# A gated linear attention followed by a feed-forward block: the same turns of 44 generators in another sequence

## The chip, the core and the metric

The kernel runs on one core of one Trainium2 chip, in one launch. Time is device microseconds of that core; lower is better. The engines are named as in the profile: PE (TensorE matmuls; PEld its weight loads), DVE (VectorE), ACT (ScalarE), POOL (GpSimd) and SP (SyncE, whose queue issues nearly all DMAs). They run unsynchronized, each through its own list of instructions in program order, and wait for one another by semaphores.

## The reference

```python
# q, k, v, alpha: (4, 8, 768, 48) = batch, heads, time, head dim
for t in range(S):
    state = alpha[:, :, t, :, None] * state + einsum('bhd,bhe->bhde', k[:, :, t], v[:, :, t])
    y[:, :, t] = einsum('bhd,bhde->bhe', q[:, :, t], state)
x = y.transpose(0, 2, 1, 3).reshape(B, S, H * D)          # (4, 768, 384)

mu, var = mean(x), variance(x)                            # over the 384 columns
xn = (x - mu) / sqrt(var + 1e-06) * g_ln
out = x + maximum(xn @ w_ch1, 0.0) @ w_ch2                # 384 -> 1536 -> 384
```

All of it is float32, but the two weight matrices arrive as 64-bit floats, which the kernel rounds on the chip.

## The kernel before

**Tiling.** Time is cut into 6 chunks of 128 steps. One attention is one chunk of one batch, so there are 24, lettered `a` to `x` (chunk 0 is `a` to `d`, chunk 5 is `u` to `x`). The gates are handled as running sums of logarithms inside a chunk (chunk 0) or half a chunk of 64 steps (the others), so that the recurrence becomes matmuls: the prefix sum (L348 for chunk 0, L355 else), exponentials of it and of its negative (L358, L359), q and k scaled by them (L363, L365), transposed by TensorE (L422, attentions `a` to `l`) or by DVE and a pass through DRAM (L404, L150, L416, `m` to `x`), the scores (L435, L450) under a mask (L459, L464), the update of the state (L479, with L488, L492 on DVE and L494 on POOL) and the output (L505, L515). Then x is stored to DRAM (L539), normalised (L543 to L557) and transposed, by TensorE (L573) for chunks 0 and 1, by DVE and DRAM else (L563, L150, L568).

In L355 each half of the time steps is one matmul of 64 rows by 64 columns of the array: an even batch sends half h to output half h, an odd batch sends the halves crosswise. The PE writes two records for one float32 matmul, so one such turn has four.

**Feed-forward.** Chunk 0 goes through plain matmuls: hidden (L598, ReLU L601) and second product (L610). Chunks 1 to 5 use a scheme with fewer block products (15 instead of 18 for each half of the hidden stage, 20 instead of 24 for the second), which needs sums of blocks made beforehand: of w1 (`combine_first`, L845), of the normalised input of a chunk (`combine_x`, L870), of w2 (`combine_weights`, L675) and of the hidden blocks (`combine_hidden`, L704). A hidden product is L901, and its results are spread by ACT copies (L913), DVE adds (L917 to L930), POOL adds (L915 to L928) and a ReLU (L932, or L940 afterwards). A product of the second stage is L722; its results go into the output tile `ob` by L736, L739, L742, L746, and `send` (L589) stores it. Some products go on accumulating in the PSUM bank of an earlier one; in the hidden stage 13 follows 1 and 0 follows 13 (`JOINS`), and the products come in the order of `FIRST`, which ends in 1, 8, 13, 4, 0. All matmul outputs share 6 PSUM banks.

**What sets the order.** Each piece of work is a Python generator that issues a few instructions and yields; such a step is one turn. A string of 1543 letters, `ORDER`, written out by hand or by a program outside the kernel, says whose turn comes next, and nothing rearranges it afterwards:

```python
with tc.manual_schedule():
    for turn in ORDER:
        next(turns[turn], None)
```

So the string fixes the order of instructions on every engine and of the DMAs on SP's queue. The letters: `a` to `x` attentions; `A` to `H` the rounding of the eight pieces of the weights (four of w1, then four of w2; a piece's last turn loads the piece after next); `Y`, `Z` the hidden stage of chunk 0, `P`, `Q` its second stage; `S`, `W`, `X`, `N` the sums of blocks of w1, w2, input and hidden; `M` the products of chunks 1 to 4 (hidden and second) and the second stage of chunk 5; `V` the hidden products of chunk 5; `R` the ReLUs; `O` the loads of x into the output tiles.

Of the kernel before, what the change touches and what calls it, by code (L numbers as in the profile page):

```python
# [25 lines left out]


ORDER = (
    "acaaababcaaabcbadbcadcaacbbbbaaabcdedcafbbcccdacbAaafebaceafcbcddcfefadebabefaAc"
    "ccdfedffcefeedffffffffddeebBbbgbhgdgghAaiabAddbdbcddhhgddidfjggYYcccgYiYYAedefcg"  # L30
    "YgjdeefeechZeiZfhijfiihhBehjBiBZihBZZhhhhhhhhhYYlZZYCfZZgfCZgZejYYiCgYkfggjfjjjj"
    "YklDZjjjjjghjkjjghkhDiihhDZZZZjlfeCgeiiehDkfikYYYYkeYlkgllEllhYighEmZlligYYkkYjh"
    "ZSYinhYSlEljnEmihlllflOnllFFjikgkZZZlZjnZZjnjFhkjjemnjfnQkGkkfegilQfSSSkGfSSlFml"
    "gkmmmPihPjlngkkmmhGglPiHSghXniQHkPXXHSSSOXllPXllooWSPppoXoSlllQjnnlnnnnoonnpSmnn"
    "mmkXOXXommXPppjmipXQnWOpOSnoQomSpWkmOmQlmSnkWnmkQMMMMMMMMiMMkMMMMMnWMMMMWpllMMMM"
    "MPMMMMnrWnpppppppppqnoMWonMrpOGrqorWWWoMrrroooMkMMWrjMMMMMMMMMMRMmMMMMRMRMqpMMjq"
    "pMOjmRnpRMMMpMiqpRqRpoRqNMoMMMtMNNRpkMNiNMMMMMnqRNmmmNMoMMMMMNNMMNsjNNNMMrqMMMMn"
    "MMMMMMoorrrprrprWrrXMpXXXXqqqqtsMNMMMpotoMNMNMXXrqrXtptmXMMMMMMMMMMMMMXXtttsMnss"
    "MMMMMsqsqsMMpsMMOMMMMMMMqrrMMMMMMMooMMRMMMqMnrMMMMMMMMMMMrRRRMMMvMMMMttOtttuqtOr"
    "tttstossrRvpnsssRRRRNvuMMMNqMMMvRMrMstrOvuNmvvtqsvrrosrtNMNNNpNrNqMMMMMMMuNssMMs"  # L40
    "ssMuurNuuMMNMMMMNOXXXXXXXtMMtMXrMXMMMxwtMMMNMNNwxtttwwwXMtMwMMMMMsMMMMMMMtMMMXMM"
    "MMMMMMMMMMMMMMMuvtqttvvvvvvvrOwvOuvwxuvuxxxquuRMMMwMMMMMMMMMMMMMMRRRMMMMMMMMMMMM"
    "MvvvqxxxxusxxxxxxRxwwwxRRRRwwMuRuqsqMMNNNMMMuuutMuuuNxxMOuwxNNxvNwwwwsNNuvvvvNNN"
    "vNvtMMMMMMMMMMMvHMMMxMXXXXXXXXXMXMMMXMMxxxMMMMNNMMwwNMMvwwwxwxxMMMMMMMMMMMMMMMMM"
    "MMMMMMMMMMMMMMMMMMMMMMMMMMMMMMxORRMMMMMMRMMMMMMMMMMMROOxxXvRRRXRRRNMXXMMMXXMMXVO"
    "NXMMMNNNNNNNNNNNXXMVVMMMMXMVVVVVVVVVVVVVVVVVVVMVVVMMMMMMMVVVVVVVVVVVVVVVVVVVMMVV"
    "VVVVVVMMMMMMMVMVVNNVVVMRNRRRRRVRRMRMMVNNOMMMMMMOMRONNNNNMNMMMMNNNMMMMOMMMMMMMNMN"
    "MMMMNMMNNMMMMMMMMMMMMMM"
)


# [951 lines left out]
```

## Time and profile before

| | before |
|---|---|
| median of 3 runs | 418.63 us |
| lowest and highest run | 416.97 and 420.4 us |
| the profiled execution, its own time | 416.17 us |
| its span, first to last instruction | 414.4 us |
| mean granted TensorE clock in it | 1.0 |
| TensorE waiting for DVE, three waits | 2.8 us |
| moved by DMA | 61.26 MB |

The profile is of one execution. A line of the timeline or of the chain begins with the start in us from the span's first instruction and a duration in us; then engine, line of the code, operation, output and inputs by the program's names, and how many instructions were merged (x4). Numbers in square brackets are the engine's idle time ahead of it and what ended it. The chain of work that ended last is followed back from the last instruction to what released it, or to the instruction before it on its engine.

### The profile page before, as it was taken

The page shows a single profiled execution, that of the slowest core. Times are in us where ns is not written, and L with a number is a line of the kernel's source. Part 1 is how long each engine was busy: PE and PEld are TensorE (multiplying, and loading weights), DVE is VectorE, ACT ScalarE, POOL GpSimd, SP SyncE. Part 2 cuts the span into 40 slices and gives each one's busy share as a digit, 9 for nine tenths or more (in the row PEclk, how much of TensorE's full clock was granted, in tenths as well). Part 3 has the DMA queues.
Part 4 walks back from the last instruction along what each step waited for, and adds up shares of the span by engine and source line. Part 5 has one row for each costly group of instructions (what it writes and reads, how often), then busy time and mean ns, then how long its engine had stood idle before and what let it go on. Part 6 is the DMA issues. An engine that isn't in the chain of part 4 may idle for free.

```text
span 414.4 us, 11452 instructions
## 1 busy us (share of the span) xinstructions
PE 408.5 (99%) x4617; PEld 354.9 (86%) x4617; DVE 292.5 (71%) x555; ACT 217.0 (52%) x521; POOL 119.7 (29%) x134
## 2 busy tenths in 40 slices
PE   7999999999999999999999999999999999999997
PEld 5878888866568889998889998899998889999996
DVE  4798989999997978597268873579533298125754
ACT  5797668783354675245684345773353643245110
POOL 1011022221012571143380254250226321525200
PEclk9999999999999999999999999999999999999999
DMA  8989959879878576946776768636234200000301
GB/s 282 292 240 278 305 125 313 237 153 264 219 138 269 133 159 116 217 106 143 168 139 160 192 165 214 122 49 137 96 62 119 68 1 2 19 0 24 111 21 58
DMA packets 134051, 61.26 MB, mean 148 GB/s; under 512 B 90559, under 2 KB 130882, under 8 KB 133998
## 3 DMA queue, kind: packets, MB, share of 16 engines
q1 hardware_dynamic: 133848, 60.37, 57.1%
q8 instruction: 36, 0.59, 0.6%
q10 hardware_dynamic: 150, 0.17, 0.1%
q14 instruction: 17, 0.14, 0.1%
HBM read 43.12 MB, written 17.39 MB: 146 GB/s over the span
## 4 chain that ended last, share of the span: by engine, by line
PE 96%; DVE 1%; DMA 1%; issue 0%; SPq 0%; DVEq 0%
PE hps L901 32%; PE ops L722 31%; PE hps L598 8%; PE ops L610 8%; PE yps L515 5%; PE tps L422 3%; PE aps L450 3%; PE ups L479 3%; PE lps L355 2%; DMA rq<-in_q_dram 1%; PE aps L435 1%; PE yps L505 1%; PE xps L573 1%; DVE eq L870 1%; PE lps L348 0%
## 5 line engine op out<-in xcount | busy, mean ns | idle before, releaser
L901 PE MATMUL hps<-sum,w 128*128 128x256 f32 x192 | 46.3, 383 | 0.0
L901 PEld LDWEIGHTS hps<-sum,w 128*128 128x128 f32 x192 | 35.7, 190 | 6.3 <-ACT u L913 1.7
L722 PE MATMUL ops<-w,hT 128*128 128x192 f32 x224 | 40.5, 326 | 0.0
L746 ACT COPY u<-ops 128x192 f32<-128x192 f32 x30 | 9.5, 316 | 54.7 <-PE ops L722 54.6
L722 PEld LDWEIGHTS ops<-w,hT 128*128 128x128 f32 x224 | 37.3, 190 | 0.3
L742 POOL TENSOR_TENSOR ob<-ob,u 128x192 f32<-128x192 f32 x32 | 20.5, 650 | 57.9 <-ACT u L746 33.1
L494 POOL TENSOR_TENSOR mid<-mid,gate 112x192 f32<-112x192 f32 x20 | 12.0, 602 | 76.8 <-DMA gate<-row 35.9
L901 PE MATMUL hps<-xT,w 128*128 128x256 f32 x136 | 33.3, 380 | 0.6 <-DVE xT L870 0.6
L598 PE MATMUL hps<-xT,w 128*128 128x256 f32 x144 | 33.8, 384 | 0.0
L913 ACT COPY u<-hps 128x512 f32<-128x512 f32 x32 | 18.7, 584 | 28.0 <-PE hps L901 22.1
L610 PE MATMUL ops<-w,hT 128*128 128x384 f32 x96 | 32.6, 491 | 0.0
L913 ACT COPY hT<-hps 128x512 f32<-128x512 f32 x40 | 23.3, 585 | 12.3 <-PE hps L901 11.9
L901 PEld LDWEIGHTS hps<-xT,w 128*128 128x128 f32 x136 | 25.7, 190 | 4.3 <-PE ops L722 0.9
L598 PEld LDWEIGHTS hps<-xT,w 128*128 128x128 f32 x144 | 26.2, 190 | 3.7 <-DVE w L258 0.2
L722 PE MATMUL ops<-ws,sum 128*128 128x192 f32 x160 | 28.6, 327 | 0.0
L610 PEld LDWEIGHTS ops<-w,hT 128*128 128x128 f32 x96 | 17.7, 190 | 11.7 <-issue 0.6
L722 PEld LDWEIGHTS ops<-ws,sum 128*128 128x128 f32 x160 | 26.4, 190 | 0.6 <-ACT few L546 0.6
L736 DVE TENSOR_TENSOR ob<-ops,ob 128x192 f32<-128x192 f32 x40 | 13.1, 351 | 17.1 <-PE ops L722 10.2
L940 ACT ACTIVATE hT<-hT 128x512 f32<-128x512 f32 x40 | 22.9, 621 | 2.0 <-DVE hT L920 1.5
L722 PE MATMUL ops<-ws,hT 128*128 128x192 f32 x128 | 23.4, 326 | 0.0
L722 PE MATMUL ops<-more,sum 128*128 128x192 f32 x120 | 22.2, 328 | 0.0
L722 PEld LDWEIGHTS ops<-ws,hT 128*128 128x128 f32 x128 | 21.3, 190 | 0.1
(225 smaller groups left out, 1028.1 us busy)
## 6 DMA issues: line engine op xcount, KB each, us to landing
ws<-in_moe_w_ch_dram SPq DMA_DIRECT2D x8, 1152.0 KB
vn<-in_v_dram SPq DMA_DIRECT2D x12, 384.0 KB
kept<-x SPq DMA_DIRECT2D x24, 192.0 KB
ob<-kept SPq DMA_DIRECT2D x24, 192.0 KB
rows<-rj SPq DMA_DIRECT2D x48, 96.0 KB
out_dram<-ob SPq DMA_DIRECT2D x18, 192.0 KB
xrows<-xt SPq DMA_DIRECT2D x64, 48.0 KB
xT<-xrows SPq DMA_DIRECT2D x16, 192.0 KB
```

Of the source, the lines that this page charges most:

```text
L422: nc.tensor.transpose(tps[:, p], qk_of(c, b)[:, i, p].rearrange("p a b -> p (a b)")[:, :R], ident)
L450: nc.tensor.matmul(pair[o][halves[i if o else 1 - i], p, s], k_of[rs, p, s], q_of[rs, p, s], start=True, stop=True)
L479: nc.tensor.matmul(up[h, p], qk_of(c, b)[ts, 1, p, i, :D], vn[ts, i, p], start=True, stop=True)
L515: nc.tensor.matmul(yps[j][halves[s], i, p], of, by, skip_group_check=True, start=not (cross and k), stop=k == 1 or not cross)
L598: nc.tensor.matmul(hps, w1[:, f, j * P:(j + 1) * P], xT_of[0][:, f, bs], start=(f == 0), stop=(f == NF - 1))
L610: nc.tensor.matmul(ops_of[b], hT_of[c][:, j, b], w2[:, j], start=(j == 0), stop=(j == NJ - 1))
L722: nc.tensor.matmul(acc, lhs[:, j], rhs[:, j], start=j == 0 and n not in FOLLOWS, stop=j == NT - 1 and n not in FOLLOWS.values(), skip_grou ...
L736: nc.vector.tensor_add(x, acc, x)
L742: getattr(nc.vector if c + 1 == NCB else nc.gpsimd, f"tensor_{op}")(x, x, y)
L901: nc.tensor.matmul(acc[:, i], w, b, start=n not in JOINS and i == 0, stop=n not in JOINS.values(), skip_group_check=True)
L913: nc.scalar.copy(out=copied[n], in_=acc)
L940: nc.scalar.activation(out=x, in_=x, func=AFT.Relu)
```

## The change

The string `ORDER` is replaced by another with the same number of every letter, so every generator issues the same instructions, in the same order within itself, on the same engines and into the same pools of buffers. What differs is how the generators' turns are interleaved, and with it the order of each engine's instructions and of the DMAs. Nothing else in the file is touched.

```diff
--- before.py
+++ after.py
@@ -26,26 +26,26 @@
 
 
 ORDER = (
-    "acaaababcaaabcbadbcadcaacbbbbaaabcdedcafbbcccdacbAaafebaceafcbcddcfefadebabefaAc"
-    "ccdfedffcefeedffffffffddeebBbbgbhgdgghAaiabAddbdbcddhhgddidfjggYYcccgYiYYAedefcg"
-    "YgjdeefeechZeiZfhijfiihhBehjBiBZihBZZhhhhhhhhhYYlZZYCfZZgfCZgZejYYiCgYkfggjfjjjj"
-    "YklDZjjjjjghjkjjghkhDiihhDZZZZjlfeCgeiiehDkfikYYYYkeYlkgllEllhYighEmZlligYYkkYjh"
-    "ZSYinhYSlEljnEmihlllflOnllFFjikgkZZZlZjnZZjnjFhkjjemnjfnQkGkkfegilQfSSSkGfSSlFml"
-    "gkmmmPihPjlngkkmmhGglPiHSghXniQHkPXXHSSSOXllPXllooWSPppoXoSlllQjnnlnnnnoonnpSmnn"
-    "mmkXOXXommXPppjmipXQnWOpOSnoQomSpWkmOmQlmSnkWnmkQMMMMMMMMiMMkMMMMMnWMMMMWpllMMMM"
-    "MPMMMMnrWnpppppppppqnoMWonMrpOGrqorWWWoMrrroooMkMMWrjMMMMMMMMMMRMmMMMMRMRMqpMMjq"
-    "pMOjmRnpRMMMpMiqpRqRpoRqNMoMMMtMNNRpkMNiNMMMMMnqRNmmmNMoMMMMMNNMMNsjNNNMMrqMMMMn"
-    "MMMMMMoorrrprrprWrrXMpXXXXqqqqtsMNMMMpotoMNMNMXXrqrXtptmXMMMMMMMMMMMMMXXtttsMnss"
-    "MMMMMsqsqsMMpsMMOMMMMMMMqrrMMMMMMMooMMRMMMqMnrMMMMMMMMMMMrRRRMMMvMMMMttOtttuqtOr"
-    "tttstossrRvpnsssRRRRNvuMMMNqMMMvRMrMstrOvuNmvvtqsvrrosrtNMNNNpNrNqMMMMMMMuNssMMs"
-    "ssMuurNuuMMNMMMMNOXXXXXXXtMMtMXrMXMMMxwtMMMNMNNwxtttwwwXMtMwMMMMMsMMMMMMMtMMMXMM"
-    "MMMMMMMMMMMMMMMuvtqttvvvvvvvrOwvOuvwxuvuxxxquuRMMMwMMMMMMMMMMMMMMRRRMMMMMMMMMMMM"
-    "MvvvqxxxxusxxxxxxRxwwwxRRRRwwMuRuqsqMMNNNMMMuuutMuuuNxxMOuwxNNxvNwwwwsNNuvvvvNNN"
-    "vNvtMMMMMMMMMMMvHMMMxMXXXXXXXXXMXMMMXMMxxxMMMMNNMMwwNMMvwwwxwxxMMMMMMMMMMMMMMMMM"
-    "MMMMMMMMMMMMMMMMMMMMMMMMMMMMMMxORRMMMMMMRMMMMMMMMMMMROOxxXvRRRXRRRNMXXMMMXXMMXVO"
-    "NXMMMNNNNNNNNNNNXXMVVMMMMXMVVVVVVVVVVVVVVVVVVVMVVVMMMMMMMVVVVVVVVVVVVVVVVVVVMMVV"
-    "VVVVVVMMMMMMMVMVVNNVVVMRNRRRRRVRRMRMMVNNOMMMMMMOMRONNNNNMNMMMMNNNMMMMOMMMMMMMNMN"
-    "MMMMNMMNNMMMMMMMMMMMMMM"
+    "acaabaabaaaccbcbbdabcaadcabbcbcdbcabecfaadaecdebeacaabfAeadcefcbbacbeffafaddbedd"
+    "fefafAdddecffbdgbbgfhfffbccgfAafbgbifAgccddbeigeadhjgghYYhBYgeidfcheAddeYfjhiceY"
+    "dchcheedgYfciidecehBdihfeZjZjZihjhhBBZBhChhhhjijjZfhjjZZfYZZlCgYfkYhgifgYkfZCeZY"
+    "geCkgYYljYfDjjgjOjkjjjghYhhZiDYkihYZkilZZkDYhYZkjSjkileifgfDiYEljlkhgEleYZlhjYgl"
+    "jfilFnYiZlgllllOEjgYlfhiFSlglgnZhZgkhnhjikFZjkkjiZPElSmhSgFfnfnnZkkghljQZSemlhGe"
+    "mSnkXGmkjkOmXlimiGQkmHSSPHQPnlPlmmHkkWlnPSolSXPOXjllXoQSXnnSoWnnSiXnnponSnXmimml"
+    "oppQjXmoQMmppMPomQMWXpkMMnkMnpMoSWMjSMnWSmPMnXmMMoOmWinMMMMllkMpMMpMnQOnkMMMMMmM"
+    "lMrMWlWMnrpMORpRkppjrpnppiprMoMqMMMMMMMrMoorWWWMMrMMoMjmlRoMMROjMMmMonMMMopRMpMM"
+    "MMRrRoRpqrlMNmNNMMMNMqqpkNqqNMqMMMpWMRNMMRMMMonMMMNqNMpMNpNqtpNWsMMXopiNMMMMMMMp"
+    "MmMMnXMrMrrrnrNrrNrqoqXtqsXrMtoXMNMXXMXMtMsotMMMMsMqtoMMXMtXMMnpMqMrMMMqXMMMMsMq"
+    "MqrMOMMMMMspmqMMMoMMsMMtMnMMMMMovMOMMMsmMMMRpsGMruqtMMqMrMqMRMMMMMMrRttrtpMtttRt"
+    "qtstORvRspRrtsouMRMNMmrMrsvMNNNvMuMMqONssMnNsrmRMsRtuuvMuotNNtpMMvuMrMMMMMNNNntM"
+    "trpvMMMsuMrMMsNMNXMMMMwMXMXNMqNXXvMMXxMuvMMNXtMwMMtXMMMMMwMwMMrtXOMwMMMMsXMMOXMw"
+    "qMMMvvtvvwvvvMvstuuuxMMrMMxMsMtMMMxMuMMwMxRORMsMMMxMMtqMMRMMsMtMMsMMMMRuMMxMRwMM"
+    "MMvMxMxuvvxxxRxOvsxxRxRNxMMwNwMMRxwNxvwwRvMNxsxxuMvMMNvwtNMNvuxMMxtNMMMNMxxMxNrM"
+    "NwwuMMNMwuxMxvMNvqXwuMXvMMMXMXMMMMMNvNwMXMMMNvuXXMXMMMMMwMMwMMMwMxMXMMMXMwuMMMMM"
+    "xMMXMMMMMMuuxMvMMwRMRMMMMMRMMMXRMMMMMuXMMMOMMMOXMMMMRMRMMMMMMMXXXXOMXRMRVMXNVXMM"
+    "VVVNVRMVNVVXRVMVNVOVVVNVVMMNVVVVVMVVNVVMVNVMMMVMVVVVNMMVVMVVMMNNRVMVVMVVNVMNMMHV"
+    "MVVMVMMMMVVRNVOVVNVVVMVMRMVMNVRMMRRRMRVNMOMOMMVNMONMMNNNRNMMMMMMMMMMRMNNNMMNMNMN"
+    "MMNMMMMNMMMMMMNMMMMMMMM"
 )
```

## The prediction

> **What bounds the kernel now.** I read the page first (busy times, then the chain that ended last), then the waits of TensorE alone, then its timeline in detail. Which engine carries the end:
>
> ```profile
> span 414.4 us, 11452 instructions
> PE 408.5 (99%) x4617; PEld 354.9 (86%) x4617; DVE 292.5 (71%) x555; ACT 217.0 (52%) x521; POOL 119.7 (29%) x134
> PE 96%; DVE 1%; DMA 1%; issue 0%; SPq 0%; DVEq 0%
> ```
>
> The last line is the chain of work that ended last: 96% of it is TensorE. "Busy" 99% alone would prove little, since matmuls overlap and their ends are modelled. So I asked whom TensorE waited for, and how long:
>
> ```profile
> PE tps L422 <- DVE qk L363: 1.1, 1, 1.1
> PE hps L901 <- DVE xT L870: 0.6, 1, 0.6
> ```
>
> (us in total, times, longest.) These are all its waits of consequence on another engine once the inputs had arrived: one before the first transposition, one late. The rest of the time it takes its turns back to back. The set of turns doesn't change, so a new order can gain little over 1.7 us in the middle and some of the start; it can lose through what TensorE pays between turns, or through new waits. Every cost below is therefore a cost per neighbour, not per instruction.
>
> **Part 1: the prefix-sum turns (L355).** For chunks 1 to 5 each attention has one such turn, 20 in all, four matmul records each. The code gives an even batch the two quarters of the array on the diagonal, an odd one the other two. In the old order most stand in pairs, even beside odd. Reading the orders turn by turn and keeping only TensorE's, the 20 turns form 12 runs before (8 pairs and 4 alone); afterwards they form 19 (1 pair, 18 alone). What a run costs, from its start to that of the next line:
>
> ```profile
> 26.22 0.86 PE L355 MATMUL lps<-la,consts 64*64 64x384 f32 x4
> 27.02 0.56 PE L479 MATMUL ups<-vn,more 128*48 128x48 f32 x16
> 27.51 0.86 PE L355 MATMUL lps<-la,consts 64*64 64x384 f32 x4
> 28.30 0.55 PE L573 MATMUL xps<-consts,xn 128*128 128x128 f32 x3
> ...
> 58.15 0.88 PE L355 MATMUL lps<-la,consts 64*64 64x384 f32 x8
> 58.84 0.57 PE L450 MATMUL aps<-qT,kT 48*64 48x64 f32 x25
> ...
> 109.07 0.88 PE L355 MATMUL lps<-la,consts 64*64 64x384 f32 x8
> 109.87 0.91 PE L610 MATMUL ops<-w,hT 128*128 128x384 f32 x2
> ```
>
> A turn alone (x4) took 0.80 and 0.79 us; a pair (x8) took 0.69 ahead of scores and 0.80 ahead of full-size matmuls. So the second turn of a pair is free, and a run costs about 0.70 whatever its length. Seven more runs: 7 x 0.70 = +4.9. The upper end is 7 x 0.80 = 5.6. For the lower end there is one turn that ran among other quarter-array work:
>
> ```profile
> 37.42 0.54 PE L355 MATMUL lps<-la,consts 64*64 64x384 f32 x2
> 37.43 0.56 PE L479 MATMUL ups<-vn,qk 64*48 64x48 f32 x6
> 37.79 0.49 PE L355 MATMUL lps<-la,consts 64*64 64x384 f32 x2
> 38.11 0.43 PE L479 MATMUL ups<-vn,qk 64*48 64x48 f32 x21
> ```
>
> Only 6 of 32 update matmuls got in beside it; that would be 6/32 of the 0.36 us that the next fence shows for a whole update turn, 0.07 saved, 7 x 0.63 = 4.4. [...] I take 4.9.
>
> **Part 2: leaving and re-entering full-array work.** The 64-row turns (update ups L479, outputs yps L515, scores aps L450, prefix sums) cost more beside full-size matmuls:
>
> ```profile
> 64.20 0.36 PE ups L479 x32
> ...
> 82.68 0.51 PE ups L479 x32
> ...
> 138.21 1.06 PE hps L901 x4
> ...
> 338.13 2.60 PE ops L722 x16
> 340.73 0.86 PE hps L901 x4
> ```
>
> This is the chain in order of time (start, us). The update took 0.36 behind another small turn, 0.51 behind a full-size one; a hidden turn took 1.06 between scores and prefix sums, 0.86 between two output products. So one excursion costs about 0.15 + 0.20 = 0.35 us. The finer mixing of hidden and output products late in the new order I cost at nothing: between these two kinds the rows show no such surcharge. Excursions number 31 before, 34 after, if the chunk-0 attention turns count as full-size, and 34 against 32 if they count as small: +1.05 or -0.7. I take +0.3.
>
> **Part 3: product 0 behind product 13.** In each half stage of hidden products, 0 accumulates in the bank of 13, which DVE must first read. With only product 4 between, TensorE waits:
>
> ```profile
> 330.36 1.03 PE L901 MATMUL hps<-xT,w 128*128 128x256 f32 x4
> 331.37 1.13 PE L901 MATMUL hps<-xT,rq 128*128 128x256 f32 x4
> ...
> 334.94 1.46 PE L722 MATMUL ops<-w,hT 128*128 128x192 f32 x8
> 337.03 1.10 PE L901 MATMUL hps<-xT,w 128*128 128x256 f32 x4 [0.63 <-DVE xT L870]
> ```
>
> 331.37 - 330.36 = 1.01 instead of 0.86: 0.15 us. The old order puts 13, 4, 0 directly after one another twice (both in chunk 4), the new one six times: +4 x 0.15 = +0.6.
>
> **Part 4: what goes.** The same fence holds the late stall. An output turn takes 1.30 (two in 2.60, above), so 334.94 should be followed at 336.24; the first hidden turn of the last chunk starts at 337.03. That is 0.8 us, waiting for the input combinations (X), which themselves began only when the transposed input of attention x had landed. In the new order 12 TensorE turns instead of 3 stand between the first X turn of that chunk and the first V turn, and 8 instead of none between x's last DMA and the X turn that reads it. The stall goes: -0.8, and nothing new is late there by this count. Kept entirely, it is 0.
>
> At the start the first transposition waits for both DVE products:
>
> ```profile
> 6.54 0.49 ACT L359 ACTIVATE lps<-lps 128x384 f32<-128x384 f32 x1
> ...
> 8.10 0.92 ACT L343 ACTIVATE la<-ra 128x384 f32<-128x384 f32 x2
> 8.37 0.65 PE L422 MATMUL tps<-consts,qk 128*112 128x128 f32 x4 [1.10 <-DVE qk L363]
> 8.86 1.46 PE L348 MATMUL lps<-la,consts 128*128 128x384 f32 x4
> ```
>
> The new order moves the logarithm of attention c ahead of b's exponentials, so it can start at 7.03 rather than 8.10 (if alpha has landed), and c's prefix sum, half of the 1.29 us that two of them take in the chain, fits into the 1.10 us gap. Between -0.65 and 0; I take -0.4.
>
> DMA issues move with their turns, past one another on SP's queue; ScalarE, DVE and GpSimd turns move too. I cost this at nothing: TensorE's work covers it. Where the cover is thinnest I count it as a rival below.
>
> **Sum**, on the profiled execution's 416.17 us (span 414.4 and 1.8 around it): 416.17 + 4.9 + 0.3 + 0.6 - 0.8 - 0.4 = 420.8. The median of the runs is 418.63 (416.97 to 420.4), so the profiled execution lies 2.5 below it, and the runs differ by 0.8%, though this trace shows no TensorE time left to lose. I read that spread as loads that are late in some runs, and let the new order's longer leads (12 turns for 3, above) absorb most of it; 0.7 of the 2.5 I leave in: 421.5.
>
> **Rivals.** (a) Lone turns cost nothing, and the spread is absorbed. [...] Then only the gains and part 3 remain: 416.17 + 0.3 + 0.6 - 1.2 = 415.9, within 414.4 to 417.5. The change then does what it says and gains some 0.6% on the median.
>
> (b) Slower than forecast: DVE becomes the bound while the weights are prepared. Its margin:
>
> ```profile
> 60.00:120.00 60.00, 60.00 (x943) 42.67 (x934) 58.48 (x98) 37.88 (x100) 10.76 (x12) 1.00 0.84 223
> 104.41 1.36 DVE L261 SCALAR_TENSOR_TENSOR w<-w,ws 128x1152 f32<-128x1152 f32 x1
> 106.29 2.85 PE L610 MATMUL ops<-w,hT 128*128 128x384 f32 x8
> ```
>
> From 60 to 120 us DVE is busy 58.48 of 60 us (fourth pair of numbers), and DMA 0.84. The last piece of w2 is ready at 105.77, and its first consumer starts at 106.29: a lead of 0.5 us. The old order has one output turn (yps) between the two, the new one none. DVE has 129 instructions ahead of that piece instead of 130, so by its own work it isn't later, and TensorE arrives later by two more prefix-sum runs (9 against 7): lead 0.5 - 1.0 + 1.4 = 0.9. If DVE idles more than 0.9 us on anything earlier (a weight load issued later, a late load), TensorE stalls by the rest. Two weight loads are indeed issued later against TensorE's work, the second and the sixth. At 3 us of such idling: 421.5 + 2.1 = 423.6, with more behind a later load; I let it reach 426.
>
> (c) The change is described as allowing for late loads and late blocks of instructions; it finds nothing to allow for: blocks weren't late, the spread of the runs has another cause and stays. Then the median is 2.5 above the sum: 423.3.
>  For it speaks "issue 0%" in the chain: in this execution no block held TensorE up. [...]
>
> **How the numbers follow.** Forecast 0.50, with its own range 419 to 422.8; (a) 0.15; (b) 0.18; (c) 0.17. The 80% range reaches from inside (a) to inside (b): 416.5 to 425.5. A measurement of this kernel can tell about 1%, that is 414.4 and 422.8. Faster by over 1% needs (a) with every gain at its best: 0.04. Slower by over 1%: (b) with 0.18, most of (c) with 0.13, and the upper edge of the forecast with 0.07: 0.38. Within 1%: 0.58.
>
> **What would show it.** Part 1: L355 in groups of four records instead of eight, each 0.7 to 0.8 us to the next start, about 5 us more of L355 in the chain; wrong if small turns start in numbers inside those 0.7 us. Part 3: gaps of 1.01 us ahead of six product-0 turns. Part 4: no wait of TensorE on L870 near 330, and a prefix sum between 7 and 8.4 us. Rival (b): a wait of L610 or the first L901 on DVE between 75 and 130 us. The forecast falls if TensorE's chain outside L355 changes by more than 2 us, or if the median lies under 417.

## The result, and the profile after

| | before | after |
|---|---|---|
| median, first comparison | 418.55 us (4 runs) | 423.64 us (4 runs, 422.46 to 424.11) |
| median, second comparison | 419.53 us (29 runs) | 423.88 us (6 runs, 422.07 to 425.73) |
| the profiled execution, its own time | 416.17 us | 424.09 us |
| span | 414.4 us | 422.1 us |

The ratio after to before is 1.0116, with an interval of 1.0068 to 1.0163, and 1.0110 (1.0072 to 1.0148) in the second comparison: slower by a little over 1%. The forecast was 421.5 with a range of 416.5 to 425.5; the time lies in the range, 2.1 us above the forecast, and just past the line that I had drawn at 1%. Three single runs among all those below (one each of before, a_new3 and b_best3) took over 1.5% longer than the fastest of their kernel; the ratios and the table by clock leave them out.

The head of the page after, the first line of its chain, and then all of TensorE's waits (us in total, times, longest):

```profile
span 422.1 us, 11463 instructions
PE 415.4 (98%) x4617; PEld 356.6 (84%) x4617; DVE 294.3 (70%) x555; ACT 213.5 (51%) x521; POOL 123.9 (29%) x134
PE 97%; DMA 1%; DVE 1%; SPq 0%; issue 0%; ACT 0%
```

```profile
PE lps L348 <- ACT la L343: 1.9, 1, 1.9
PE lps L283 <- DVE more L280: 1.0, 1, 1.0
PE hps L901 <- DVE xT L870: 0.7, 1, 0.7
```

TensorE still carries the chain, and it has 6.9 us more busy time (415.4 against 408.5) with the same 4617 matmul records. So most of what was added isn't waiting; it is time that TensorE takes for the same work in another neighbourhood and, at the start, at a lower clock (0.50 from 9.00 to 12.40 us). Where most of it sits is shown by the groups by line (last columns: busy us, mean ns of one, idle before). Before, then after:

```profile
L355 PE MATMUL lps<-la,consts 64*64 64x384 f32 x80 | 10.4, 503 | 0.0
```

```profile
L355 PE MATMUL lps<-la,consts 64*64 64x384 f32 x80 | 16.3, 497 | 0.0
L348 PE MATMUL lps<-la,consts 128*128 128x384 f32 x8 | 4.8, 692 | 1.9 <-ACT la L343 1.9
```

The 80 records of the prefix sums cover 5.9 us more, although one record lasts no longer (497 ns against 503): fewer of them run beside one another. What follows them, in the timeline of after (start, us):

```profile
157.95 0.84 PE L355 MATMUL lps<-la,consts 64*64 64x384 f32 x4
158.72 1.13 PE L901 MATMUL hps<-xT,rq 128*128 128x256 f32 x4
```

```profile
61.09 0.54 PE L355 MATMUL lps<-la,consts 64*64 64x384 f32 x2
61.11 0.33 PE L450 MATMUL aps<-qT,kT 48*64 48x64 f32 x4
61.46 0.49 PE L355 MATMUL lps<-la,consts 64*64 64x384 f32 x2
61.78 1.10 PE L450 MATMUL aps<-qT,kT 48*64 48x64 f32 x60
```

Ahead of full-size work a lone turn costs 0.77 us. Ahead of scores it is split into its two halves, and a few score matmuls start inside (here 4 of 64, since 60 come behind it), so a little of the 0.69 us is given back.

The start differs as well. ScalarE (ACT) and TensorE of after, then the windows of after and of before from 9 to 12.4 us (the number ahead of the last two is the granted clock of TensorE):

```profile
8.19 0.52 ACT L343 ACTIVATE la<-ra 128x384 f32<-128x384 f32 x1 [1.39 <-DMA ra<-in_alpha_dram]
8.77 1.50 PE L348 MATMUL lps<-la,consts 128*128 128x384 f32 x2 [1.88 <-ACT la L343]
10.06 1.92 PE L422 MATMUL tps<-consts,qk 128*112 128x128 f32 x8
```

```profile
9.00:12.40 3.40, 3.40 (x12) 2.39 (x12) 2.17 (x4) 2.17 (x6) 0.00 (x0) 0.50 0.96 327
```

```profile
9.00:12.40 3.40, 3.40 (x31) 2.64 (x31) 2.09 (x4) 2.22 (x6) 0.00 (x0) 1.00 1.09 365
```

The gates of attention c land at 8.2 us, TensorE waits 1.88 us for them ahead of the first transposition, and then runs at half clock (0.50): 12 matmul records in 3.4 us where before, with other turns in that place, had 31. And the late stall that was to go is still there, 0.72 us:

```profile
338.83 1.13 PE L901 MATMUL hps<-xT,rq 128*128 128x256 f32 x4
339.55 0.42 DVE L870 TENSOR_TENSOR eq<-eq 128x256 f32<-128x256 f32 x1
339.79 1.46 PE L722 MATMUL ops<-w,hT 128*128 128x192 f32 x8
340.00 1.84 DVE L870 TENSOR_TENSOR xT<-xT,eq 128x256 f32<-128x256 f32 x2
340.23 1.32 POOL L927 TENSOR_TENSOR hT<-hT,u 128x512 f32<-128x512 f32 x1 [1.21 <-ACT u L913]
341.98 1.10 PE L901 MATMUL hps<-xT,w 128*128 128x256 f32 x4 [0.72 <-DVE xT L870]
```

The sums for the last chunk overwrite the transposed input of chunk 4, which the hidden turn at 338.83 is the last to read. They start at 340.00, when that turn has ended (339.96) and DVE is through with the sum ahead of them (339.97), and two of them take 1.84 us, while TensorE has one product turn to go on with. The second alone takes 1.38 us, beside a GpSimd addition (L927). At the 0.42 us of the first it would have ended at about 340.9, ahead of the end of TensorE's product turn (339.79 + 1.30 = 341.09). So the stall needs both, the short lead and the slow sum.

### The profile page after: what moved, and what is told of

Same layout as the page of the kernel before. It is cut to its first block, busy times and chain, and to the rows that moved or that the text cites. A ratio compares the mean times of both kernels' runs of the same rounds, so it can differ in the third digit from the quotient of the medians.

```text
span 422.1 us, 11463 instructions
## 1 busy us (share of the span) xinstructions
PE 415.4 (98%) x4617; PEld 356.6 (84%) x4617; DVE 294.3 (70%) x555; ACT 213.5 (51%) x521; POOL 123.9 (29%) x134
## 4 chain that ended last, share of the span: by engine, by line
PE 97%; DMA 1%; DVE 1%; SPq 0%; issue 0%; ACT 0%
PE hps L901 32%; PE ops L722 31%; PE hps L598 8%; PE ops L610 8%; PE yps L515 5%; PE lps L355 3%; PE tps L422 3%; PE aps L450 3%; PE ups L479 2%; DMA ra<-in_alpha_dram 1%; PE aps L435 1%; PE yps L505 1%; PE xps L573 1%; PE lps L348 1%; DVE xT L870 0%; SPq L166 0%
## 5 line engine op out<-in xcount | busy, mean ns | idle before, releaser
L901 PE MATMUL hps<-sum,w 128*128 128x256 f32 x192 | 46.9, 384 | 0.0
L901 PEld LDWEIGHTS hps<-sum,w 128*128 128x128 f32 x192 | 35.4, 190 | 6.6 <-ACT u L913 1.9
L494 POOL TENSOR_TENSOR mid<-mid,gate 112x192 f32<-112x192 f32 x20 | 13.8, 691 | 81.3 <-DVE mid L492 46.4
L901 PE MATMUL hps<-xT,w 128*128 128x256 f32 x136 | 33.7, 380 | 0.7 <-DVE xT L870 0.7
L598 PE MATMUL hps<-xT,w 128*128 128x256 f32 x144 | 33.8, 383 | 0.0
L598 PEld LDWEIGHTS hps<-xT,w 128*128 128x128 f32 x144 | 26.3, 190 | 5.0 <-issue 0.6
L901 PEld LDWEIGHTS hps<-xT,w 128*128 128x128 f32 x136 | 25.6, 190 | 4.1 <-PE ops L722 1.0
L494 POOL TENSOR_TENSOR st<-st,gate 112x192 f32<-112x192 f32 x16 | 13.9, 871 | 42.4 <-DVE st L492 42.4
L547 ACT ACTIVATE xn<-x,few 128x384 f32<-128x384 f32 x24 | 14.8, 615 | 20.0 <-DVE few L543 18.5
```

Of the source, the lines that this page charges most:

```text
L494: nc.gpsimd.tensor_mul(new, new, by)
L547: act(out=xn, in_=x, func=AFT.Square, bias=mean, accum_out=dev)
L598: nc.tensor.matmul(hps, w1[:, f, j * P:(j + 1) * P], xT_of[0][:, f, bs], start=(f == 0), stop=(f == NF - 1))
L901: nc.tensor.matmul(acc[:, i], w, b, start=n not in JOINS and i == 0, stop=n not in JOINS.values(), skip_group_check=True)
```

## The experiments

Theory 1: a run of prefix-sum turns costs TensorE its price whether it has one turn or two, because the two of a pair use different quarters of the array. Theory 2: the runs differ because TensorE is sometimes granted half clock after its gap at the start. Theory 3: the late stall is the wait just shown. The rivals stand in each expectation. All kernels but four differ from before or after in ORDER alone; diffs of it show the line or the letters moved.

**Joining all pairs (a_pairs).** Each of the 20 prefix-sum turns of after next to its neighbour batch's. Where a turn could not be moved alone, the steps that depend on it moved along, up to seven turns of an attention:

```diff
-    "jfilFnYiZlgllllOEjgYlfhiFSlglgnZhZgkhnhjikFZjkkjiZPElSmhSgFfnfnnZkkghljQZSemlhGe"
+    "jfilFnYiZlgllllOEjgYlfhiFSlglgZhZgkhhjikFZjkkjiZPElSmhSgFffZkkghljQZSenmnnnnlhGe"
...
```

> The kernel after, with each of the 20 prefix-sum turns of chunks 1 to 5 put next to the one of its neighbour batch: 10 runs of two instead of 19. Theory 1 (a run costs TensorE about 0.70 us whether it has one turn or two): 9 x 0.70 = 6.3 us less than after, about 417.3, with L355 in the trace near 7.5 us instead of 12. Rival A (the added time comes from the late start and other waits, and a lone prefix sum is filled by small work behind it): within 1.5 us of after, 422 to 424. Rival B (every excursion from full-size to small work costs, and 33 excursions stay about 33): no change either.

Measured: 430.63 us, ratio 1.0257 (1.0211 to 1.0303). Both the theory and the rivals missed. L355 fell from 16.3 to 9.4 us busy, as theory 1 wants, and the time rose by 7 us. Its waits of TensorE say why:

```profile
PE tps L422 <- DVE qk L363: 4.0, 1, 4.0
PE lps L348 <- ACT la L343: 2.2, 1, 2.2
PE ops L610 <- DVE qk L363: 1.8, 1, 1.8
PE xps L573 <- DVE xn L553: 1.2, 1, 1.2
```

The steps held back are exponentials and scalings, so DVE's products (L363) come late for TensorE, once by 4.0 us. DVE as the bound, my rival (b), didn't strike in after, but this order runs into it. The experiment doesn't decide theory 1; a smaller one was needed.

**Joining five pairs that stand close (a_pairs2).** Only prefix-sum turns move, no other step:

```diff
-    "dchcheedgYfciidecehBdihfeZjZjZihjhhBBZBhChhhhjijjZfhjjZZfYZZlCgYfkYhgifgYkfZCeZY"
-    "geCkgYYljYfDjjgjOjkjjjghYhhZiDYkihYZkilZZkDYhYZkjSjkileifgfDiYEljlkhgEleYZlhjYgl"
+    "dchcheedgYfciidecehBdihfeZjZjZihjhhBBZBhChhhhjijjZfhjjZZfYZZlCgYfkYhgifgYklfZCeZ"
+    "YgeCkgYYjYfDjjgjOjkjjjghYhhZiDYkihYZkilZZkDYhYZkjSjkileifgfDiYEljlkhgEleYZlhjYgl"
...
```

> The kernel after with only those five pairs of prefix-sum turns joined whose turns stood at most 3 TensorE turns apart, or whose second had its gates ready long before (e with f, k with l, s with t, u with v, w with x); no other step of an attention moves. 14 runs instead of 19. Theory 1: 5 x 0.70 = 3.5 us less than after, about 420.1, with each joined run of eight records 0.69 to 0.80 us long. Rival A (joining them makes other work wait, as in the kernel with all ten joined, which took 430.6): no gain, 423 to 425.

Measured: 421.07 us (419.55 to 423.36), ratio to before 1.0044 (1.0013 to 1.0075), where after has 1.0110 to 1.0116. That is 0.7% or 2.8 us less than after, 0.56 a run instead of 0.70. Compared with after's trace record by record, the first four joins bring what follows them forward by 0.78, 0.61, 0.59 and 0.61 us. The fifth (w with x) brings 0.12, since the scores behind it wait 0.3 us for DVE (L930). The group of L355 in this kernel:

```profile
L355 PE MATMUL lps<-la,consts 64*64 64x384 f32 x80 | 11.8, 496 | 0.0
```

**Splitting seven pairs in the kernel before (b_lone).** The second turn of each pair goes behind the next TensorE turn, for instance q behind o:

```diff
-    "MPMMMMnrWnpppppppppqnoMWonMrpOGrqorWWWoMrrroooMkMMWrjMMMMMMMMMMRMmMMMMRMRMqpMMjq"
+    "MPMMMMnrWnpppppppppqnoMWonMrpOGroqrWWWoMrrroooMkMMWrjMMMMMMMMMMRMmMMMMRMRMqpMMjq"
...
```

> The kernel before, with 7 of its 8 pairs of prefix-sum turns broken: the second of each goes behind the next TensorE turn, 19 runs instead of 12 as in after. Loads, weights and everything else stand as before. Theory 1: 7 x 0.70 = +4.9 us, about 423.5, all of it in L355 and the turn behind it. Rival A (prefix sums cost nothing alone, the rest of the new order does it): within 1 us of before, 418 to 420.

Measured: 423.42 us (420.44 to 424.33), ratio 1.0086 (1.0052 to 1.0121), +3.6 us by the ratio (the medians differ by 4.5), 0.51 a run. L355 covers 4.4 us more than in before (10.4):

```profile
L355 PE MATMUL lps<-la,consts 64*64 64x384 f32 x80 | 14.8, 501 | 0.0
```

The average hides two kinds. Compared with before's trace record by record, five of the seven splits cost 0.59 to 0.97 us each, and two, at 61.87 and 80.79 us, cost 0.05 or less: the second turn of the pair, moved behind a turn of scores, still started 0.18 us after the first, with four score matmuls between. Rival A falls: nothing else of the new order is in this kernel, and it has most of after's loss.

**Same quarters for both turns (b_same).** In the kernel before, an odd batch's prefix sum takes the diagonal quarters too:

```diff
-                of = halves[1 - h if b % 2 else h]
+                of = halves[h]
```

> The kernel before, where odd batches also take the two quarters on the diagonal, so that their prefix sum covers the other half of the chunk (the output differs from the reference; instructions, sizes and order stay). What it tells apart is why the second turn of a pair is free. Theory 1a (the two turns of a pair run beside each other in different quarters): each of the 8 pairs takes about twice as long, +8 x 0.65 = +5.2 us, about 423.7, and a run of eight records lasts 1.4 us to the next start instead of 0.7. Rival 1b (a run pays a fixed price for leaving and re-entering full-array work, and the turns themselves are short): no change, 418 to 419.5, eight records still in 0.7 us.

Measured: 423.36 us, ratio 1.0081 (1.0051 to 1.0110), +3.4 us. One run of eight records ahead of product turns, in before and then here:

```profile
177.27 0.84 PE L355 MATMUL lps<-la,consts 64*64 64x384 f32 x8
178.04 0.76 PE L722 MATMUL ops<-ws,sum 128*128 128x192 f32 x3
```

```profile
182.74 1.47 PE L355 MATMUL lps<-la,consts 64*64 64x384 f32 x8
184.14 1.08 PE L722 MATMUL ops<-ws,sum 128*128 128x192 f32 x5
```

0.77 us became 1.40 us for the same eight records in the same place. So the pair is cheap because its turns run in different quarters (1a), not because a visit to small work has a fixed price (1b). Record by record against before's trace, each of the eight pairs costs 0.60 to 0.65 us, 5.0 in sum where 5.2 was expected. The measured 3.4 us is less than that; why isn't shown, but before's usual runs lose time that its profiled one does not (the table below and the section on the prediction).

**The first hidden turn of the last chunk one product later (a_vlate).**

```diff
-    "xMMXMMMMMMuuxMvMMwRMRMMMMMRMMMXRMMMMMuXMMMOMMMOXMMMMRMRMMMMMMMXXXXOMXRMRVMXNVXMM"
+    "xMMXMMMMMMuuxMvMMwRMRMMMMMRMMMXRMMMMMuXMMMOMMMOXMMMMRMRMMMMMMMXXXXOMXRMRMVXNVXMM"
```

> The kernel after, with the first hidden turn of the last chunk one product later: product turn 362 now stands ahead of it. Theory 3 (the late stall is the wait for two sums that cannot start before the last hidden product of chunk 4 has read the input they overwrite, then 0.43 + 1.39 us of DVE against one product of 1.46 us on TensorE): 0.7 us less, about 422.9, and no wait of TensorE for L870. Rival (the sums are late through the load of x, which landed at 331): the wait stays near 0.7, since the load has long landed it would be elsewhere; the time is unchanged.

Measured: 421.66 us (421.35 to 425.39), ratio 1.0068 (1.0032 to 1.0104). That is 2.0 us less than after where 0.7 was expected, but the interval overlaps after's, and seven of its ten runs had the full clock where five of after's ten had it (the table below). So the size rests on the trace. There the wait is gone, with DVE as slow as in after:

```profile
338.45 1.46 PE L722 MATMUL ops<-w,hT 128*128 128x192 f32 x8
338.65 1.84 DVE L870 TENSOR_TENSOR xT<-xT,eq 128x256 f32<-128x256 f32 x2
339.75 1.46 PE L722 MATMUL ops<-ws,hT 128*128 128x192 f32 x8
341.05 1.03 PE L901 MATMUL hps<-xT,w 128*128 128x256 f32 x4
```

This shows that one more product covers the two sums. It doesn't tell apart what holds their start, the buffer that they overwrite or their place in DVE's list, since both came free together in after.

**Keeping TensorE busy at the start (b_warm, a_warm).** Six matmuls on zeros fill its gap; before: ahead of the first transposition, after: ahead of c's prefix sum. The diff is that of b_warm; in a_warm the same matmuls stand ahead of L348, for attention c alone:

```diff
+        if c + b == 0:
+            for _ in range(6):
+                nc.tensor.matmul(idle[:, :P], zero, zero, start=True, stop=True)
         for i in () if turned(c, b) else (1, 0):
```

> The kernel before with six small matmuls on zeros (as those of L283, into the same unused tile) put on TensorE ahead of the first transposition, where it idles from about 7.2 to 8.4 us. Theory 2 (the runs differ because TensorE, after an idle stretch of 1 to 2.5 us there, is sometimes granted half clock from about 8 to 12 us; nothing later differs): every run has clock 1.0, none is above 419, the median falls from 418.9 to about 417.6, the lowest run stays at 417. Rival C (the spread comes from loads and instruction blocks that arrive late at random): the spread stays at 417 to 422, and the median at 418.9 or up to 0.5 more for the added matmuls.

> The kernel after with the same six matmuls ahead of the third prefix sum of chunk 0, where it waits from about 6.8 to 8.7 us for the gates of attention c. Theory 2: every run has clock 1.0, the runs lie within 1.2 us of the lowest, the median falls from 423.6 to about 422.4; so only about 1.2 of the 5.1 us between the kernels is the start. Rival C: the runs keep their spread of 422.4 to 424.1 or more, and clock 0.995 stays in most.

Measured: b_warm 418.93 us (418.1 to 421.4, 12 runs), ratio 0.9992 (0.9964 to 1.0021); a_warm 423.45 us (422.63 to 424.3, 6 runs), ratio 1.0092 (1.0056 to 1.0127). The clock did as theory 2 says: all 18 runs have 0.999 or 1.0, where 11 of the 29 runs of before beside them have 0.996 or less. It isn't a full cure: of the twelve runs of b_best2 below, which has the same six matmuls, two still have 0.995 and 0.996. And the medians did not follow. b_warm's lowest run is 1.2 us above before's, its median 0.9 above that of before's runs at the same clock (418.0), and its waits show a second cause:

```profile
PE lps L283 <- DVE more L280: 1.1, 1, 1.1
PE hps L601 <- issue: 0.7, 1, 0.7
PE hps L904 <- issue: 0.7, 1, 0.7
```

TensorE twice stood still for 0.7 us with nothing that the profile shows to wait for, at 41.39 us and at 218.46 us (the lines are three further on by the insertion: L601 is L598, L904 is L901). Rival C isn't refuted, then: besides the clock such gaps make runs differ too, though no run shows what causes them. Whether the 24 more records on TensorE made these two gaps likelier isn't shown; b_best2, with the same matmuls, has gaps at the same two places (0.5 and 0.3 us).

**The early prefix sum of c, alone (b_start).** The kernel before with c's gates and prefix sum where after has them:

```diff
-    "acaaababcaaabcbadbcadcaacbbbbaaabcdedcafbbcccdacbAaafebaceafcbcddcfefadebabefaAc"
+    "acaaababcaaacbbcadbadcaacbbbbaaabcdedcafbbcccdacbAaafebaceafcbcddcfefadebabefaAc"
```

> The kernel before with the gates (Ln) and the prefix sum of attention c as early as in after: ahead of the first transposition. My step 4 had it fit into the gap for nothing (0.4 gained): 418.3. Theory 2 (the gates of c land at 8.2 us or later, so TensorE waits for them and the first transposition comes 0.4 to 1 us later, and the half clock strikes as often or more often): 419.2 to 420, with a wait of L348 for the gates of 1.5 to 2.6 us in place of the wait of L422 for DVE.

Measured: 418.94 us (416.74 to 421.89), ratio 0.9995 (0.9967 to 1.0023). The wait came as expected, on the gates, but no loss that can be measured, and no gain either. The half clock, going by a mean clock of 0.992 to 0.996, struck less often than expected, in two of the twelve runs against 16 of the 29 of before beside them; at clock 0.999 or 1.0 the median is 418.8. The waits of its profile on the gates:

```profile
PE lps L348 <- ACT la L343: 2.6, 2, 2.2
```

**All repairs together, and the kernel before mended (a_new3, b_best3); after once more.** a_new3 has the moves of a_pairs2 and a_vlate and c's start as in before. b_best3 is before with the first hidden turn (V) of the last chunk one product later, and h's prefix sum directly behind g's:

```diff
-    "ccdfedffcefeedffffffffddeebBbbgbhgdgghAaiabAddbdbcddhhgddidfjggYYcccgYiYYAedefcg"
+    "ccdfedffcefeedffffffffddeebBbbgbhghdggAaiabAddbdbcddhhgddidfjggYYcccgYiYYAedefcg"
...
-    "MMMMMMMMMMMMMMMMMMMMMMMMMMMMMMxORRMMMMMMRMMMMMMMMMMMROOxxXvRRRXRRRNMXXMMMXXMMXVO"
-    "NXMMMNNNNNNNNNNNXXMVVMMMMXMVVVVVVVVVVVVVVVVVVVMVVVMMMMMMMVVVVVVVVVVVVVVVVVVVMMVV"
+    "MMMMMMMMMMMMMMMMMMMMMMMMMMMMMMxORRMMMMMMRMMMMMMMMMMMROOxxXvRRRXRRRNMXXMMMXXMMXON"
+    "XMMVMNNNNNNNNNNNXXMVVMMMMXMVVVVVVVVVVVVVVVVVVVMVVVMMMMMMMVVVVVVVVVVVVVVVVVVVMMVV"
```

> The kernel after with the three repairs that the runs so far support, and nothing else: the five pairs of prefix-sum turns joined, the first hidden turn of the last chunk one product later, and the gates and the prefix sum of attention c put back to where the kernel before has them. Theory 1 plus theory 3 plus the start: 3.5 + 0.7 + 0.3 less than after's 423.6, about 419.1, within 1 us of before; no wait of TensorE for L870 and none of L348 for the gates of c. Rival (what is left of the difference is something else in the new order, spread over many places): above 420.5.

> The kernel before with two small moves: the prefix sum of h right behind that of g (11 runs instead of 12), and the first hidden turn of the last chunk one product later. By the terms 0.70 + 0.63 less than before: about 417.5, with no wait of TensorE for L870 late. Rival: nothing to be gained, since a late instruction block or the half clock at the start fills what is freed: 418.5 to 419.

> The kernel after once more, unchanged, for its spread. If the half clock at the start is what divides the runs: two groups, about 422.3 where the mean granted clock is 1.0 or 0.999 and about 424 where it is 0.995 or 0.996; kernel before alike, about 417.7 and 420. Compared within a group, after is 4.3 us slower in both.

Measured, beside before's 419.53 us: a_new3 419.82 (ratio 1.0015, 0.9988 to 1.0043), b_best3 417.84 (0.9962, 0.9931 to 0.9993), after once more 423.88. The three repairs take after back to before, within the interval. At equal clock (the table below) 0.6 to 1.5 us is left; two more runs of prefix sums than in before (14 against 12) would be 1.1 of it at 0.56 each, and in its profile the joined pair of e and f took 1.46 us, since f's gates came late. What is left can thus be turns that stay alone, but that isn't tested apart. b_best3 beats both kernels by a little. Its waits no longer have L870. The join of g and h brought nothing: its eight records took 1.62 us to the next start, as much as the two turns alone, because the second turn's weight load had to wait for h's gates:

```profile
28.34 1.70 PE L355 MATMUL lps<-la,consts 64*64 64x384 f32 x8
29.17 0.20 PEld L355 LDWEIGHTS lps<-la,consts 64*64 64x64 f32 x4 [0.64 <-ACT la L343]
29.96 0.56 PE L479 MATMUL ups<-vn,more 128*48 128x48 f32 x16
```

One more kernel, b_best2: as b_best3, with i's prefix sum held back to j's besides, the turns of the other pairs put side by side in `ORDER` where turns without TensorE stood between, and the six matmuls at the start:

> The kernel before with the last lone prefix-sum turns joined too (g with h, i with j: 10 runs instead of 12), the first hidden turn of the last chunk one product later, and the six matmuls of the run above at the start. By the terms: 2 x 0.70 + 0.6 for the stall + 1.3 for the clock at the start = 3.3 us less than before, about 415.6. Rival A (moving the prefix sum of i behind eight TensorE turns makes its scores wait for DVE): 417 to 419.

Measured: 418.58 us (418.05 to 421.32), ratio 0.9990 (0.9965 to 1.0015). No gain: its profile has new waits of TensorE of 0.4 to 0.6 us (for a weight piece, for x transposed, for a load of kT) and 0.8 us for "issue". The wait of the scores of i for DVE, which rival A named, isn't among them.

The runs by granted clock, medians in us (number of runs). Before's come from the three comparisons that the experiments were part of, and the kernels ran on more than one chip; before's own median at full clock was 418.2, 418.4 and 417.5 in the three comparisons, so differences under 1 us mean little here:

| kernel | clock 0.999 or 1.0 | clock 0.991 to 0.996 |
|---|---|---|
| before | 418.0 (45) | 420.2 (36) |
| after | 422.7 (5) | 424.4 (5) |
| b_lone | 421.5 (4) | 424.0 (6) |
| b_same | 421.8 (3) | 423.7 (6) |
| a_pairs2 | 419.8 (4) | 421.6 (6) |
| a_vlate | 421.5 (7) | 422.9 (3) |
| a_new3 | 419.5 (8) | 420.8 (3) |
| b_best3 | 417.2 (9) | 418.9 (2) |

At equal clock after is 4.7 and 4.2 us slower than before. The two groups are 1.4 to 2.5 us apart in every kernel: one stretch of 3.4 us at half clock, as in the windows above, would cost about half of it, an estimated 1.7.

## Why the prediction was right in kind and 2.1 us low

**Part 1, prefix sums: the mechanism is shown, the size was at the upper end.** Two experiments in opposite directions price a run at 0.51 (b_lone) and 0.56 us (a_pairs2) on average, and b_same shows the quarters as the cause. By these prices seven runs cost 3.6 to 3.9 us, not 4.9. The traces put it somewhat higher. From start to start, the records of L355 take 3.4 us more in after than in before (11.99 against 8.63 us). The matmuls that started inside its turns hold another 1.7 us (2.10 against 0.36), part of which they would have needed anyway. So 4.9 was at most 1.3 us too much. I had taken the price from turns ahead of full-size work and had given the inside of a lone turn to no one; scores (4 of 64 at 61.11 us in after), and updates as well (6 of 32 at 37.43 us in before), do start between its two halves, and a split pair can still run side by side (0.18 us apart at 61.87 and 80.79 us in b_lone). Lone turns that cost nothing, the premise of rival (a), no run shows: seven more runs cost 0.51 us each in b_lone, and five fewer gave back 0.56 each in a_pairs2. So its 415.9 was out of reach.

**Part 2, excursions: +0.3, not tested alone.** The matmuls of the scores take 1.5 us more in after by start-to-start times (11.86 against 10.37 for L450). Of these, 0.9 are scores that started inside a lone prefix sum, so they belong to Part 1; the rest is only argued.

**Part 3, product 0 behind 13: seen, not tested.** Six hidden turns are followed at 1.01 or 1.02 us, as at 338.83 after 337.81, where before had two: 4 x 0.15. All hidden turns of chunks 1 to 5 together take 1.3 us more in after (133.7 against 132.4 from start to start), so about as much again lies in other neighbourhoods of theirs.

**The three parts together.** Leaving out waits and the lines of the start (L283, L319, L348, L422), TensorE's work takes 5.5 us more from start to start in after's trace than in before's. The three terms came to 4.9 + 0.3 + 0.6 = 5.8.

**Part 4, the late stall: wrong.** The step that failed is the count of twelve turns between the first X turn and the first V turn. The V turn doesn't read the first sum but the sixth, which overwrites the old transposed input. That one can't start before the last hidden product of chunk 4, and between that product and the V turn the new order has one product turn. The lead that decides is from the last reader of the buffer, not from the first turn of the letter; and the 1.38 us of the slow sum made that lead too short. a_vlate shows that one product more is enough. The load of x, to which I had put the stall down, had landed at 331.04 in after. In before it wasn't the load either: DVE went into these sums at 332.09 without a wait, straight from L920, and the first two took 2.34 us.

**Part 4, the start: no gain.** I had let the logarithm of c begin at 7.03 us "if alpha has landed". It lands at 8.2. b_start bounds the effect between -1.4 and +1.0 us. After's profiled start was 2.1 us longer than before's (L348 and L422 together 18.4 against 16.2 us, start to start). Of these, 0.8 is the longer wait (1.88 against 1.10); the rest fits the granted clock of that execution (0.50 from 9.00 to 12.40 us).

**Rival (b)** did not happen: TensorE has no wait on DVE between 75 and 130 us in after.

**What made the number low.** I had set the terms on the profiled execution, 416.17, and left 0.7 of the 2.5 us up to the median, expecting the new order to absorb the rest. That execution was a lucky one: the lowest of 82 later runs is 416.71. Two steps failed. The gains of Part 4, 1.2 us, did not come; without them the same sum gives 422.7, which is the median of after's five runs at clock 0.999 or 1.0. And the half clock at the start, going by a mean clock of 0.992 to 0.996, is in the other five of after's ten runs, as in rival (c), which has the spread stay and whose 423.3 is within 0.6 us of both measured medians. After's two groups of runs are 1.7 us apart.

Rival (c) is only half right, though, for what isn't the clock did shrink. At clock 0.999 or 1.0, before's 45 runs lie between 416.7 and 421.0 us, after's five between 422.1 and 423.4, and the seven of a_vlate, of nearly the same order, between 421.4 and 422.0. The profiles show one cause of before's larger spread. In three of the seven in before's order (b_warm, b_best3, b_start) ScalarE's logarithm for the second turn of the pair near 140 us waits for a DMA, and TensorE loses 0.4 to 0.8 us there. In b_warm:

```profile
141.00 0.52 ACT L343 ACTIVATE la<-ra 128x384 f32<-128x384 f32 x1 [1.87 <-DMA xrows<-xt]
141.58 0.14 PEld L355 LDWEIGHTS lps<-la,consts 64*64 64x64 f32 x2 [0.66 <-ACT la L343]
```

Before's own profile doesn't have this wait, nor have the six in after's order (a_pairs aside). So the spread has at least three sources: the half clock at the start, the gaps for "issue", and DMAs that end late. The new order doesn't cure the first. For the second, TensorE stood still once for "issue" in after's second profile, 0.2 us. Of the third it has less, as I had let it, but by how much isn't measured.

**Where luck comes in.** The difference of the medians is 4.4 to 5.1 us and the terms came to +4.6, but the agreement is luck. By the traces, parts 1 to 3 alone came to 5.5, and the gains of 1.2 did not come. What makes up for it must lie in before's usual runs, whose median at full clock is 1.8 us above the profiled execution (418.0 against 416.17); of these 1.8 us only the pieces named above are seen.

## What to carry to other kernels

Put work that fills half the array beside work for the other half (eight records of L355 took 0.77 us so, and 1.40 us in the same quarters), and when reordering count the neighbours lost; but join such turns only where nothing else has to be held back for it (a_pairs took 7 us more). Read a lead from the last reader of the buffer that is overwritten, not from the load or from the first step of a stage. Make a sum of changes against the median of the runs, not against one profiled execution that may be the luckiest, and compare runs of the same granted clock (the two groups are 1.4 to 2.5 us apart here).

## What the hardware showed that I had not expected

**Gaps for "issue", multiples of 256 records apart.** In 14 profiled executions TensorE stood still for "issue" ten times for 0.15 us or more, at most 0.98. Counting all its records (matmuls, weight loads and the waits between them, by start) up to each gap gives 449 twice, 705 once, 1217 five times and 6081 twice: 193 + 256 n every time, with n = 1, 2, 4, 23. The longest, in b_lone, behind 1217 records:

```profile
45.61 0.49 PE L422 MATMUL tps<-consts,more 128*112 128x128 f32 x3 [0.98 <-issue]
```

An execution has some 9,320 such records, so an estimated 36 such places, and eight of the 14 profiles, those of before and after among them, show no gap at any. In the windows around record 1217 DMA was busy for 0.83 to 1.02 of its time, around the other five 0.30 to 0.99, so busy DMA alone doesn't explain them; the cause stays open.

**Half clock after some short gaps.** TensorE idled 0.6 to 3.1 us at about 8 us in the 14 profiles. With 1.3 us or less (four executions) the clock stayed at 1.0 there. With 1.7 us or more, six of ten then ran at half clock for some 3.4 us (0.50 from 9.00 to 12.40 us in after, 0.51 in b_best3), and four, with 2.2, 2.2, 2.6 and 3.1 us, did not; one of these four, a_pairs, had its stretch at 35.2 us, in a gap of 4.0 us. So half clock followed gaps of 1.7 us (b_same, b_best3, after_again) and did not follow one of 3.1 us (a_new3); what decides isn't shown.

**Sums on DVE three times slower beside GpSimd.** The two sums at 340.00 in after take 0.42 and 1.38 us, and the next one 1.37, where the same kind takes 0.42 us at 339.55; the slow ones lie under the POOL additions L927 and L928. The slow one of the two ends at 341.84, 0.3 us behind the end of L927 (341.55). In the traces of before and after together, the 77 sums of L870 that overlap no POOL instruction take 0.38 to 0.43 us and the 33 others 0.41 to 1.49, so not all beside GpSimd are slow; why some are isn't shown. In a_vlate the two take the same 1.84 us and cost nothing, since one more product covers them.
